# Attention, gated network and relu6 network in one kernel: attention steps placed later and closer in the first block, and x's loads and result copies reordered in the second network

## The chip, the cores and the metric

The kernel runs on one core of one Trainium2 chip. The metric is device microseconds (us) of that core; the kernel before has a median of 1795.02 us over three runs (1794.77 to 1796.37).

A core has five engines that each run their own list of instructions in order and wait for each other through semaphores: TensorE (PE: matmuls, and PEld, its weight loads), VectorE (DVE), ScalarE (ACT), GpSimd (POOL) and SyncE (SP, which here only issues transfers). The profile gives TensorE's granted clock as a share of full speed.

## The reference

Three stages follow each other on 4608 tokens of 512 features:

```
attention: 8 batches, 8 heads, 576 tokens, 64 features a head, in chunks of 64 tokens
  s = q_c @ k_c.T / 8 ;  p = exp(s - max(s)) ;  p = p / (sum(p) + 1e-9) ;  x = p @ v_c
first network (d_ff 1536):
  xn = x / sqrt(mean(x*x) + 1e-6) * rms_g
  y  = (silu(xn @ w_gate) * (xn @ w_val)) @ w_out
second network (d_ff 2048):
  h = y @ w_in ;  out = (h * clip(h + 3, 0, 6) / 6) @ w_out
```

All inputs are float32. Each product is made of three matmuls on split operands (high part times high part, low times high, high times low), so that the result keeps nearly the accuracy of float32.

## The kernel before

The tokens are cut into nine blocks of 512. **The first network** runs over the blocks b = 0 to 8, and in each over twelve steps f of 128 hidden features. A step has three parts: the gate product (`mm_up` into PSUM bank 2, 12 matmuls, then silu on ScalarE into the one buffer `sg`), the value product (`mm_up` into bank 3, then VectorE multiplies it into `sg`, L890, and `split_act` makes the high part `ah` on ScalarE, L746, and the low part `al` on GpSimd, L747), and the down product of the step before (`mm_down_a`, 12 matmuls into banks 4 to 7, of which the last four, L720, read `al`). After each part a counter `hk` (0 to 35) goes up, and two hooks are called with it: `att_hook` and `prep_hook`.

`att_hook` places the attention of the next block, two halves of 256 tokens (class `Pair`), one after the other: `turn` (two transposes of q and k on VectorE), `scores` (TensorE), `top` and `less` (VectorE), `expo` (ScalarE), `total` (VectorE), `share` (GpSimd), `trans_p` (TensorE), `out_p` (ScalarE), `values` (TensorE), `out_x` and `square` (ScalarE) and `squares` (VectorE). When both halves are done, `rms` norms the block, and at the block's end `x_split` writes the high and low parts XH and XL for the next block. In later blocks a half takes five steps f. In block 0 the same distances are kept, one step later: the first half stands at hk 4 to 16 (steps 2 to 6, counted from 1), the second at hk 19 to 31, and `rms` at hk 34.

`prep_hook` prepares in block 0 the 36 weight pieces of the first network. Every second hk issues one stage for two pieces at a time (`Prep.step`): on VectorE the last operation of one group (`lo`, L171) and eight operations of the next (`bits`, L147, L149, L151, L155, two each), on ScalarE a cast and an absolute value (`hi`, L162, `mag`, L140). A stage stands on VectorE directly behind what the hook before it issued. In later blocks the weights of the second network are prepared instead, at a slower pace (`Stash.step`).

**The second network** takes block 0 alone and then pairs of blocks (1 and 2, 3 and 4, 5 and 6, 7 and 8). A pair needs seven sums and differences of its x, each as high and low part (the `xo` tiles, made from `x4` by `x_fill`: four subtractions `xt` on VectorE, then for each operand a cast on ScalarE, L932, and a subtraction on VectorE, L935). `x_fill` is a generator with two rounds c = 0 and 1, which use one buffer `x4` in turn; `go(fill, n)` runs it up to its n-th `yield`. The products of a pair come in eight iterations i (42 matmuls each, L704). While one block's down products of these iterations are collected in one half of PSUM, the gated values of the other block are kept; when the eight are done, two last down products for the first block follow, its results are scaled and copied out (`o_store`, one half by ScalarE, one by VectorE, L761), and sixteen down products for the second block (`mm_down_b`, 12 matmuls each, whose operands `split_act` makes one or two products ahead) run while `x_fill` prepares the next pair. All transfers of x and of the results, and the stream of stored weights (`stream.ahead`), are issued in order by SyncE.

Of the kernel before, what the change touches and what calls it, by code (L numbers as in the profile page):

```python
# [17 lines left out]
def _f32_of(word):  # L18
# [18 lines left out]
    square3 mean2 spread1 norm1 spread0 root2 squares3 mean3 wl2 inv2 root3 wh3 hi1 spread2 norm0 inv3 wm5  # L37
    norm2 hi2 lo1 spread3 hi0 lo2 norm3 hi3 lo3 wh4 wm6 lo0 wl3 wb5 wb6 wh5 wl4
""".split()
STEPS_A = range(0, 36, 2)  # L40


@with_exitstack
def fused_kernel(
# [13 lines left out]
    nc = tc.nc  # L58
# [6 lines left out]
    N = 512  # L65
    NB = NT // N
# [4 lines left out]
    NQ = FB // 2  # L71
# [431 lines left out]
    TP = 256  # L503
# [250 lines left out]
            nc.vector.tensor_copy(t[:, 1, :], PS[:, YB + m + 1, :])  # L754
            nc.sync.dma_start(out=yd[b][:, m:m + 2, :], in_=t)

    def o_store(b, base=YB):
        for m in range(0, NTL, 2):
            t = st_p.tile([128, 2, DM], F32, tag="st", name="ost")
            for z, e in ((0, nc.scalar.mul), (1, nc.vector.tensor_scalar_mul)):  # L760
                e(t[:, z, :], PS[:, base + m + z, :], 1.0 / 6.0)  # L761
                r = b * N + (m + z) * 128
                if b == NB - 1:
                    nc.sync.dma_start(out=out[r:r + 128, :], in_=t[:, z, :])
            r = b * N + m * 128
            if b < NB - 1:
                nc.sync.dma_start(out=out[r:r + 256, :].rearrange("(m p) d -> p m d", p=128), in_=t)
# [11 lines left out]
    with tc.manual_schedule():  # L779
# [38 lines left out]
        def att_hook(b, hk):  # L818

            if b + 1 >= NB:  # L820
                return
            f, o = divmod(hk, 3)
            a = state["att"]
            if b == 0:
                if hk == 0:
                    a.load_v()
                f -= 1
            t, g = divmod(f, 5)
            if t < 0:
                return  # L830
            if t == N // TP:
                if o == 1 and g == 0:
                    rms(b + 1)
                return
            if (g, o) == (0, 1):
                a.run("turn")
                if a.i + 1 < NPR:
                    state["nxt"] = Pair(a.i + 1)
                    if b == 0:
                        state["parts"] = state["nxt"].parts_qk()  # L840
                    else:
                        state["nxt"].load_qk()
            elif (g, o) == (1, 0):
                a.run("scores")
            elif (g, o) == (1, 1):
                a.run("top", "less", "expo")
            elif (g, o) == (2, 1):
                a.run("total", "share")
            elif (g, o) == (3, 1):
                a.run("trans_p", "out_p")  # L850
            elif (g, o) == (4, 1):
                a.run("values", "out_x", "square", "squares")
                if "nxt" in state:
                    state["att"] = state.pop("nxt")
                    state["att"].load_v()

# [56 lines left out]
        def x_fill(b):  # L913

            for j in range(7):
                if j not in X:
                    X[j] = [wp.tile([128, 2, N], F32R, tag="w", name="xo") for _ in range(2)]
            for c in range(2):
                x4 = xf_p.tile([128, KD, N], F32, tag="xf", name="x4")
                nc.sync.dma_start(out=x4[:, 0:2, :], in_=yd[b][:, c:c + 3:2, :])  # L920
                nc.sync.dma_start(out=x4[:, 2:4, :], in_=yd[b + 1][:, c:c + 3:2, :])
                yield
                x11, x21, x12, x22 = (x4[:, z, :] for z in range(4))
                src = {B11: x11, B21: x21, B22: x22}
                for j, p, m in ((T1, x12, x11), (T2, x22, T1), (T3, x22, x12), (T4, x21, T2)):
                    src[j] = tmp_p.tile([128, N], F32, tag="tmp", name="xt")
                    nc.vector.tensor_tensor(src[j], p, src[m] if m in (T1, T2) else m, op=ALU.subtract)  # L927
                    if j == T2 or j == T4:
                        yield
                for j in range(8):  # L930
                    if j < 7:
                        nc.scalar.copy(X[j][0][:, c, :], src[j])  # L932
                    if j > 0:
                        hi, lo = X[j - 1]
                        nc.vector.tensor_tensor(  # L935
                            lo[:, c, :], src[j - 1], hi[:, c, :].bitcast(F32), op=ALU.subtract
                        )
                    yield
# [19 lines left out]
        def relu(r, h):  # L958
            nc.scalar.activation(r, h, AF.Relu, bias=three)
# [29 lines left out]
        for b in range(1, NB, 2):  # L989
# [3 lines left out]
            for i in range(NQ):  # L993
                f0, f1 = 2 * i, 2 * i + 1
                t = [stream.t[i, k_] for k_ in range(4)]
                p0, p1, p2, p3 = (PS[:, base + z, :] for z in range(4))
                add = nc.vector.tensor_tensor
                product(base, t[0][:, 0], X[B11])
                u1 = temp("u1")
                nc.scalar.copy(u1, p0)  # L1000
                product(base + 1, t[0][:, 1], X[T2])
                u2 = temp("u2")
                add(u2, u1, p1, op=ALU.add)  # L1003
                product(base + 2, t[1][:, 1], X[T3])
                u3 = temp("u3")
                add(u3, u2, p2, op=ALU.add)
                product(base + 3, t[1][:, 0], X[T1])
                c22 = temp("c22")
                add(c22, u3, p3, op=ALU.add)
                r22 = g_tile(f1)  # L1010
                relu(r22, c22)
                add(u2, u2, p3, op=ALU.add)
                product(base, t[2][:, 0], X[B21])
                add(u1, u1, p0, op=ALU.add)
                r11 = sg_p.tile([128, N], F32, tag="sg", name="sg")
                relu(r11, u1)
                product(base + 1, t[3][:, 1], X[T4])
                gate(r22, c22)
                add(u3, u3, p1, op=ALU.add)
                r21 = at_p.tile([128, N], F32, tag="sqs", name="r21")  # L1020
                relu(r21, u3)
                product(base + 2, t[2][:, 1], X[B22])
                stream.ahead(4)
                gate(r11, u1)
                add(u2, u2, p2, op=ALU.add)
                r12 = g_tile(f0)
                relu(r12, u2)
                if prev is not None:
                    for z in range(2):
                        mm_down_b(W["out2", f0 - 2 + z], prev[z], i == 1 and z == 0, False, base=yb)  # L1030
                gate(r21, u3)
                gate(r12, u2)
                prev = [split_act(r11), split_act(r21)]
            fill = x_fill(b + 2) if b + 2 < NB else iter(())
            nx = []
            for z in range(2):
                mm_down_b(W["out2", FB - 2 + z], prev[z], False, z == 1, base=yb)
                nx.append(split_act(g_tile(z)))
            o_store(b, yb)
            for f in range(FB):  # L1040
                if 0 < f < FB - 1:
                    nx.append(split_act(g_tile(f + 1)))
# [35 lines left out]
```

## Time and profile before

| | |
|---|---|
| profiled execution | 1796.53 us, its span 1794.7 us |
| runs | 1795.02 us median of 3 |
| granted TensorE clock, mean | 0.984 |
| TensorE matmuls busy | 1729.3 us, 96% of the span |
| VectorE busy | 881.4 us, 49% |
| ScalarE busy | 643.5 us, 36% |
| GpSimd busy | 495.1 us, 28% |
| transfers, share of 16 engines | 31.7% and 7.1% on the two large queues |

The span cut into 40 equal slices (45 us each), as the page prints them: TensorE is at nine tenths or more from the fifth slice on, and below it only in the first four, in which VectorE stands at seven and eight tenths, and the granted clock at seven tenths in the first two.

```
PE   5698999999999999999999999999999999999999
DVE  7886554445455444644542243544554454454440
PEclk7799999999999999999999999999999999999999
```

A row of a timeline gives the start, the length, the engine, the line of the kernel, the operation, what it writes and reads, how many instructions were merged, and in brackets how long the engine stood idle before it and what ended that idle time. Matmuls overlap: one takes 0.39 us as recorded, and the next starts 0.23 us after it.

### The profile page before, as it was taken

What the parts mean: (1) busy time and instruction counts of PE and PEld (TensorE: products, weight loads), DVE (VectorE), ACT (ScalarE), POOL (GpSimd) and SP (SyncE); (2) the same over time, 40 slices, a digit from 0 to 9 for tenths busy, and PEclk for the clock granted to TensorE, in tenths of its full rate; (3) what the DMA queues carried; (4) which work ended last, traced back from release to release, by engine and by line L of the source; (5) the groups of instructions that cost most, each with busy time, mean ns of one, the idle gap of its engine ahead of it and who ended that gap; (6) DMA issues with size and microseconds to landing.
All of it is one profiled execution on the core that took longest, in us unless ns stands there. A gap on an engine that the chain in (4) does not pass through costs nothing.

```text
span 1794.7 us, 24671 instructions
## 1 busy us (share of the span) xinstructions
PE 1729.3 (96%) x9664; PEld 1417.1 (79%) x9664; DVE 881.4 (49%) x1186; ACT 643.5 (36%) x971; POOL 495.1 (28%) x359
## 2 busy tenths in 40 slices
PE   5698999999999999999999999999999999999999
PEld 4577788888888888888888888887788778878887
DVE  7886554445455444644542243544554454454440
ACT  5453333343333333334332133333333333333332
POOL 2321232323323232332333232112421321142123
PEclk7799999999999999999999999999999999999999
DMA  9831342423424133342317354444244334424410
GB/s 268 227 68 29 84 110 69 117 55 97 106 71 125 51 95 95 85 113 77 92 42 262 142 205 147 164 141 141 70 164 141 114 103 141 142 88 141 141 63 32
DMA packets 273589, 207.17 MB, mean 115 GB/s; under 512 B 196289, under 2 KB 233153, under 8 KB 273345
## 3 DMA queue, kind: packets, MB, share of 16 engines
q1 hardware_dynamic: 240704, 163.65, 31.7%
q10 hardware_dynamic: 32768, 41.95, 7.1%
q8 instruction: 76, 1.25, 0.3%
q14 instruction: 41, 0.33, 0.1%
HBM read 161.48 MB, written 44.04 MB: 115 GB/s over the span
## 4 chain that ended last, share of the span: by engine, by line
PE 86%; DVE 6%; DMA 4%; issue 1%; SPq 1%; ACT 1%; POOL 0%; DVEq 0%; POOLq 0%
PE PS L693 32%; PE PS L704 17%; PE PS L725 6%; PE PS L726 6%; PE PS L729 6%; PE PS L717 5%; PE PS L718 5%; PE PS L720 5%; DMA x<-yd 2%; DVE xo L935 1%; PE PS L569 1%; PE PS L629 1%; DVE xt L927 1%; DMA wraw<-in_moe_w_val_dram 1%; PE PS L611 1%
## 5 line engine op out<-in xcount | busy, mean ns | idle before, releaser
L747 POOL TENSOR_TENSOR al<-sg,ah 128x512 fp32r<-128x512 f32 x156 | 213.7, 1370 | 1023.0 <-ACT ah L746 716.1
L693 PE MATMUL PS<-XH,w 128*128 128x512 f32 x1728 | 439.1, 397 | 9.3 <-DVE sg L890 3.2
L693 PEld LDWEIGHTS PS<-XH,w 128*128 128x128 f32 x1728 | 328.1, 191 | 81.9 <-DVE sg L890 3.9
L704 PE MATMUL PS<-xo,wq 128*128 128x512 f32 x1344 | 309.2, 389 | 0.0
L704 PEld LDWEIGHTS PS<-xo,wq 128*128 128x128 f32 x1344 | 252.3, 188 | 52.4
L890 DVE TENSOR_TENSOR sg<-sg,PS 128x512 f32<-128x512 f32 x108 | 74.1, 686 | 336.2 <-PE PS L693 332.2
L725 PE MATMUL PS<-w,ah 128*128 128x512 f32 x576 | 225.2, 391 | 10.7 <-ACT ah L746 10.7
L693 PE MATMUL PS<-XL,w 128*128 128x512 f32 x864 | 233.6, 392 | 0.0
L726 PE MATMUL PS<-w,ah 128*128 128x512 f32 x576 | 224.2, 389 | 0.0
L746 ACT CAST ah<-sg 128x512 fp32r<-128x512 f32 x156 | 96.8, 621 | 293.1 <-DVE sg L890 249.4
L693 PEld LDWEIGHTS PS<-XL,w 128*128 128x128 f32 x864 | 164.2, 190 | 35.3 <-POOL XL L495 0.6
L717 PE MATMUL PS<-ah,w 128*128 128x512 f32 x432 | 174.8, 405 | 0.0
L718 PE MATMUL PS<-ah,w 128*128 128x512 f32 x432 | 168.3, 390 | 0.0
L729 PE MATMUL PS<-w,al 128*128 128x512 f32 x576 | 154.5, 389 | 0.0
L885 ACT ACTIVATE sg<-PS 128x512 f32<-128x512 f32 x108 | 64.5, 597 | 229.3 <-PE PS L693 176.6
L725 PEld LDWEIGHTS PS<-w,ah 128*128 128x128 f32 x576 | 108.1, 188 | 36.8 <-ACT ah L746 14.5
L729 PEld LDWEIGHTS PS<-w,al 128*128 128x128 f32 x576 | 107.8, 188 | 23.0 <-POOL al L747 0.6
L726 PEld LDWEIGHTS PS<-w,ah 128*128 128x128 f32 x576 | 108.1, 188 | 22.3
L720 PE MATMUL PS<-al,w 128*128 128x512 f32 x432 | 115.6, 389 | 1.3 <-POOL al L747 1.3
L1003 DVE TENSOR_TENSOR u<-u,PS 128x512 f32<-128x512 f32 x32 | 22.0, 688 | 156.7 <-PE PS L704 147.6
L717 PEld LDWEIGHTS PS<-ah,w 128*128 128x128 f32 x432 | 81.1, 188 | 18.8 <-issue 1.9
L720 PEld LDWEIGHTS PS<-al,w 128*128 128x128 f32 x432 | 81.0, 188 | 18.5 <-POOL al L747 1.7
(135 smaller groups left out, 1937.3 us busy)
## 6 DMA issues: line engine op xcount, KB each, us to landing
wq<-stash_in SPq DMA_DIRECT2D x152, 512.0 KB, 3.7
yd<-yst SPq DMA_DIRECT2D x18, 512.0 KB, 3.0
sraw<-in_moe_w_in_dram ACTq DMA_DIRECT2D x16, 512.0 KB, 4.7
stash_in<-slo ACTq DMA_DIRECT2D x32, 256.0 KB, 2.9
sraw<-in_moe_w_out_dram ACTq DMA_DIRECT2D x16, 512.0 KB, 5.8
w<-stash_out SPq DMA_DIRECT2D x16, 512.0 KB, 4.1
x<-yd SPq DMA_DIRECT2D x16, 512.0 KB, 5.6
out_dram<-ost SPq DMA_DIRECT2D x16, 512.0 KB, 3.2
```

Of the source, the lines that this page charges most:

```text
L693: nc.tensor.matmul(ps, w(wi, c), xs[c][xi], start=(i == 0), stop=(i == n - 1))
L704: nc.tensor.matmul(PS[:, bank, :], op[:, wi, c * 128:(c + 1) * 128], x[xi][:, c, :], start=(i == 0), stop=(i == 5),)
L717: nc.tensor.matmul(ps, wm[0], a[0], start=first, stop=False)
L718: nc.tensor.matmul(ps, wm[1], a[0], start=False, stop=False)
L720: nc.tensor.matmul(PS[:, YB + m, :], w[:, 0, m * 128:(m + 1) * 128], a[1], start=False, stop=last)
L725: nc.tensor.matmul(PS[:, base + m, :], am, w[:, 0, :], start=first, stop=False)
L726: nc.tensor.matmul(PS[:, base + m, :], am, w[:, 1, :], start=False, stop=False)
L729: nc.tensor.matmul(PS[:, base + m, :], a[1][:, m * 128:(m + 1) * 128], w[:, 0, :], start=False, stop=last)
L746: nc.scalar.copy(hi, t)
L747: nc.gpsimd.tensor_tensor(lo, t, hi.bitcast(F32), op=ALU.subtract)
L885: nc.scalar.activation(s, PS[:, GB, :], AF.Silu)
L890: nc.vector.tensor_tensor(s, s, PS[:, VB, :], op=ALU.mult)
```

## The change

In block 0 a table by hk takes the place of the shifted distances: the first half of the attention stands at hk 13 to 20 and the second at hk 22 to 29, each step as far from the next as the table says, and `rms` at hk 31, where later blocks have it. The later blocks keep their places (`LATER` is the old chain of conditions as a table). The loads of the following half's q and k, which the hook starts at `turn`, and of v, at `squares`, move with them.

In the second network the generator for the next pair is made before the last down products of iteration i = 7, and run once, so that SyncE issues the loads of round 0 there, behind the stream's loads and ahead of the results' transfers. Round 1 rests five more yields between its load and its first subtraction. `o_store` of the first block of a pair makes all four copies on VectorE.

```
+FIRST = {
+    13 + 9 * t + d: steps
+    for t in range(2)
+    for d, steps in (
+        (0, ("turn",)),
...
+        (7, ("values", "out_x", "square", "squares")),
+    )
+}
+FIRST[31] = ("rms",)
...
-    def o_store(b, base=YB):
+    def o_store(b, base=YB, engines=(nc.scalar, nc.vector)):
         for m in range(0, NTL, 2):
             t = st_p.tile([128, 2, DM], F32, tag="st", name="ost")
-            for z, e in ((0, nc.scalar.mul), (1, nc.vector.tensor_scalar_mul)):
-                e(t[:, z, :], PS[:, base + m + z, :], 1.0 / 6.0)
+            for z, e in enumerate(engines):
+                mul = e.mul if e is nc.scalar else e.tensor_scalar_mul
+                mul(t[:, z, :], PS[:, base + m + z, :], 1.0 / 6.0)
...
             if b == 0:
                 if hk == 0:
                     a.load_v()
-                f -= 1
-            t, g = divmod(f, 5)
...
+                due = FIRST.get(hk, ())
+            else:
+                f, o = divmod(hk, 3)
+                t, g = divmod(f, 5)
+                due = LATER.get((g, o), ()) if t < N // TP else ("rms",) if (g, o) == (0, 1) else ()
+            for step in due:
+                if step == "rms":
                     rms(b + 1)
+                    continue
+                a.run(step)
+                if step == "turn" and a.i + 1 < NPR:
                     state["nxt"] = Pair(a.i + 1)
...
                 nc.sync.dma_start(out=x4[:, 2:4, :], in_=yd[b + 1][:, c:c + 3:2, :])
-                yield
+                for _ in range(1 + 5 * c):
+                    yield
...
                 r12 = g_tile(f0)
                 relu(r12, u2)
+                if i == NQ - 1:
+                    fill = x_fill(b + 2) if b + 2 < NB else iter(())
+                    go(fill, 1)
                 if prev is not None:
...
-            fill = x_fill(b + 2) if b + 2 < NB else iter(())
             nx = []
             for z in range(2):
                 mm_down_b(W["out2", FB - 2 + z], prev[z], False, z == 1, base=yb)
                 nx.append(split_act(g_tile(z)))
-            o_store(b, yb)
+            o_store(b, yb, (nc.vector, nc.vector))
```

What stands on VectorE in block 0 from the multiply of step 2 on, before (L890 is the multiply, L556 and L557 the transposes of `turn`, L171 to L155 one preparation stage of two pieces):

```order
L890 TENSOR_TENSOR sg<-sg,PS 128x512
L556 STREAM_TRANSPOSE qT<-q 128x1024
L557 STREAM_TRANSPOSE kT<-k 128x1024
L171 TENSOR_TENSOR w<-wraw,w 128x512 x2
L147 TENSOR_SCALAR wtmp<-wtmp 128x512 x2
L149 TENSOR_SCALAR wtmp<-wtmp 128x512 x2
L151 SCALAR_TENSOR_TENSOR wtmp<-wraw,wtmp 128x512 x2
L155 SCALAR_TENSOR_TENSOR wraw<-wraw,wtmp 128x512 x2
```

The same place in the changed kernel, where the multiply is L902 and the stage L193 to L177, up to the multiply of step 3:

```order
L902 TENSOR_TENSOR sg<-sg,PS 128x512
L193 TENSOR_TENSOR w<-wraw,w 128x512 x2
L169 TENSOR_SCALAR wtmp<-wtmp 128x512 x2
L171 TENSOR_SCALAR wtmp<-wtmp 128x512 x2
L173 SCALAR_TENSOR_TENSOR wtmp<-wraw,wtmp 128x512 x2
L177 SCALAR_TENSOR_TENSOR wraw<-wraw,wtmp 128x512 x2
L193 TENSOR_TENSOR w<-wraw,w 128x512 x2
L169 TENSOR_SCALAR wtmp<-wtmp 128x512 x2
L171 TENSOR_SCALAR wtmp<-wtmp 128x512 x2
L173 SCALAR_TENSOR_TENSOR wtmp<-wraw,wtmp 128x512 x2
L177 SCALAR_TENSOR_TENSOR wraw<-wraw,wtmp 128x512 x2
L902 TENSOR_TENSOR sg<-sg,PS 128x512
```

The transposes are gone from here: two stages stand directly behind the multiply of step 2. The same holds at step 4, where `total` stood between the multiply and two stages, and at step 3, where `top` and `less` stood before one stage.

On VectorE around `total` of the first half, before (L597 to L600 are `total`, then two stages, of which the second is cut here, up to the multiply of step 5):

```order
L597 TENSOR_REDUCE sm<-p 128x16
L598 TENSOR_SCALAR sm<-sm 128x16
L600 RECIPROCAL rs<-sm 128x16
L171 TENSOR_TENSOR w<-wraw,w 128x512 x2
L147 TENSOR_SCALAR wtmp<-wtmp 128x512 x2
L149 TENSOR_SCALAR wtmp<-wtmp 128x512 x2
L151 SCALAR_TENSOR_TENSOR wtmp<-wraw,wtmp 128x512 x2
L155 SCALAR_TENSOR_TENSOR wraw<-wraw,wtmp 128x512 x2
```

Now (L619 to L622 are `total`, L674 is `squares` of the same half):

```order
L619 TENSOR_REDUCE sm<-p 128x16
L620 TENSOR_SCALAR sm<-sm 128x16
L622 RECIPROCAL rs<-sm 128x16
L193 TENSOR_TENSOR w<-wraw,w 128x512 x2
L169 TENSOR_SCALAR wtmp<-wtmp 128x512 x2
L171 TENSOR_SCALAR wtmp<-wtmp 128x512 x2
L173 SCALAR_TENSOR_TENSOR wtmp<-wraw,wtmp 128x512 x2
L177 SCALAR_TENSOR_TENSOR wraw<-wraw,wtmp 128x512 x2
L902 TENSOR_TENSOR sg<-sg,PS 128x512
L674 TENSOR_REDUCE sqs<-kT 128x256
```

Between `total` and `squares` stood three stages and two multiplies; now one stage and one multiply stand there, and `share`, `trans_p`, `out_p`, `values`, `out_x` and `square` on the other engines have that much time.

On SyncE at the end of a pair's iterations (here blocks 3 and 4), before (L324 is the stream of stored weights, L767 the results, L920 and L921 the loads of x):

```order
L324 DMA wq<-stash_in_108 128x1024 x4
L324 DMA wq<-stash_in_111 128x1024 x2
L767 DMA out_dram<-ost 128x2x512 x2
L920 DMA x_11324<-yd_104 128x2x512
L921 DMA x_11324<-yd_105 128x2x512
L920 DMA x_11429<-yd_104 128x2x512
```

Now (L346 the stream, L932 and L933 the loads of x, L790 the results):

```order
L346 DMA wq<-stash_in_108 128x1024 x4
L346 DMA wq<-stash_in_111 128x1024 x2
L932 DMA x_11250<-yd_104 128x2x512
L933 DMA x_11250<-yd_105 128x2x512
L790 DMA out_dram<-ost 128x2x512 x2
L932 DMA x_11429<-yd_104 128x2x512
```

The two loads of round 0 have moved in front of the results' transfers, and follow the stream's loads at once.

## Rows read from the trace of the kernel before

**Rows 1.** TensorE by stretch: length, busy and matmuls, granted clock, transfers' share, GB/s
```profile
55.60:190.10 134.50, 117.55 (x706) 0.92 0.38 94
1123.53:1142.57 19.04, 19.04 (x86) 1.00 0.64 221
1243.21:1291.24 48.03, 44.55 (x193) 1.00 0.21 66
1410.93:1459.43 48.50, 44.56 (x194) 1.00 0.21 66
1579.11:1626.91 47.80, 44.53 (x194) 1.00 0.21 66
```

**Rows 2.** TensorE's waits: line, releaser, us in total, times, longest
```profile
PE PS L725 <- ACT ah L746: 10.7, 9, 1.5
```

**Rows 3.** Timeline of TensorE in block 0 and at the start of block 1
```profile
81.77 1.98 PE L569 MATMUL PS<-kT,qT 64*64 64x64 f32 x64 [3.21 <-DVE kT L557]
...
115.19 3.61 PE L693 MATMUL PS<-XH,w 128*128 128x512 f32 x8 [3.15 <-DVE sg L890]
...
139.99 1.99 PE L569 MATMUL PS<-kT,qT 64*64 64x64 f32 x64 [5.27 <-DVE kT L557]
...
190.10 0.50 PE L693 MATMUL PS<-XH,w 128*128 128x512 f32 x1 [2.02 <-ACT XH L682]
...
199.46 1.98 PE L693 MATMUL PS<-XH,w 128*128 128x512 f32 x8
```

**Rows 4.** Timeline of VectorE in block 0
```profile
68.42 1.28 DVE L171 TENSOR_TENSOR w<-wraw,w 128x512 fp32r<-128x512 f32 x2
...
72.17 1.29 DVE L155 SCALAR_TENSOR_TENSOR wraw<-wraw,wtmp 128x512 uint32<-128x512 uint32 x2
75.25 0.69 DVE L890 TENSOR_TENSOR sg<-sg,PS 128x512 f32<-128x512 f32 x1 [1.78 <-ACT sg L885]
75.85 1.24 DVE L556 STREAM_TRANSPOSE qT<-q 128x1024 f32<-128x1024 f32 x1
...
92.10 1.22 DVE L579 TENSOR_REDUCE mx<-PS 128x16 f32<-128x1024 f32 x1
93.36 1.29 DVE L589 TENSOR_TENSOR p<-PS,mx 128x512 f32<-128x512 f32 x2
...
100.56 1.21 DVE L597 TENSOR_REDUCE sm<-p 128x16 f32<-128x1024 f32 x1
...
102.90 2.93 DVE L171 TENSOR_TENSOR w<-wraw,w 128x512 fp32r<-128x512 f32 x2
...
114.46 0.68 DVE L890 TENSOR_TENSOR sg<-sg,PS 128x512 f32<-128x512 f32 x1
...
125.11 2.06 DVE L652 TENSOR_REDUCE sqs<-kT 128x256 f32<-128x1024 f32 x1 [2.52 <-ACT kT L649]
```

**Rows 5.** Timeline of GpSimd in block 0
```profile
69.24 5.35 POOL L747 TENSOR_TENSOR al<-sg,ah 128x512 fp32r<-128x512 f32 x1 [9.99 <-ACT ah L746]
76.67 1.30 POOL L747 TENSOR_TENSOR al<-sg,ah 128x512 fp32r<-128x512 f32 x1 [2.09 <-ACT ah L746]
...
103.06 2.22 POOL L605 TENSOR_TENSOR p<-p,rs 128x1024 f32<-128x1024 f32 x1 [0.40 <-DVE rs L600]
```

**Rows 6.** Timeline of ScalarE in block 0, and in the second network at blocks 1 and 2
```profile
77.60 1.21 ACT L140 ACTIVATE wtmp<-wraw 128x512 f32<-128x512 f32 x2
...
1251.20 0.62 ACT L932 CAST xo<-x 128x512 fp32r<-128x512 f32 x1 [5.30 <-DMA x<-yd]
```

**Rows 7.** Timeline of SyncE's issues in block 0, and in the second network
```profile
138.84 16.25 SPq L537 DMA_DIRECT2D q<-in_q_dram  x32
...
1210.76 22.55 SPq L324 DMA_DIRECT2D wq<-stash_in  x8
...
1244.76 0.79 SPq L920 DMA_DIRECT2D x<-yd  x1
```

**Rows 8.** Timeline of VectorE in the second network, at the first subtraction of x
```profile
1252.58 1.67 DVE L927 TENSOR_TENSOR xt<-x 128x512 f32<-128x512 f32 x1 [8.33 <-DMA x<-yd]
```

More of the change, by code (lines that the diff above doesn't have):

```diff
@@ L39 @@
 """.split()
+FIRST = {
[3 more added lines that the diff above has]
+        (0, ("turn",)),
+        (2, ("scores",)),
+        (3, ("top", "less", "expo")),
+        (4, ("total", "share")),
+        (6, ("trans_p", "out_p")),
+        (7, ("values", "out_x", "square", "squares")),
+    )
+}
+FIRST[31] = ("rms",)
+LATER = {
+    (0, 1): ("turn",),
+    (1, 0): ("scores",),
+    (1, 1): ("top", "less", "expo"),
+    (2, 1): ("total", "share"),
+    (3, 1): ("trans_p", "out_p"),
+    (4, 1): ("values", "out_x", "square", "squares"),
+}
 STEPS_A = range(0, 36, 2)
@@ L821, in att_hook @@
                 return
-            f, o = divmod(hk, 3)
             a = state["att"]
@@ L826, in att_hook @@
                     a.load_v()
-                f -= 1
-            t, g = divmod(f, 5)
[L829 to L832, printed above, removed]
+                due = FIRST.get(hk, ())
[5 more added lines that the diff above has]
+                if step == "rms":
                     rms(b + 1)
[L834 to L837, printed above, removed]
+                    continue
+                a.run(step)
+                if step == "turn" and a.i + 1 < NPR:
                     state["nxt"] = Pair(a.i + 1)
@@ L842, in att_hook @@
                         state["nxt"].load_qk()
[L843 to L853, printed above, removed]
+                elif step == "squares" and "nxt" in state:
                     state["att"] = state.pop("nxt")
```

## The prediction, made blind

> **What bounds the kernel now.** I read the stretches of TensorE first, then its waits, then the timelines of the engines that it waits for. TensorE is busy nearly all the time, so a gain is there only where it stands or runs slowly. In undisturbed work 84 matmuls take 19.04 us, 0.2267 us each (the second stretch of [rows 1], which counts two overlapping neighbours with them). Two places fall short of that.
>
> The first is block 0. Its 36 products of 12 matmuls are 432 x 0.2267 = 97.9 us, and the stretch takes 134.5 at a mean granted clock of 0.92 [rows 1]. TensorE stands 3.21 and 5.27 us for the transposed k, 3.15 us for a multiply and 2.02 us for XH at the start of block 1 [rows 3]. After each of the four the clock is at its lower level for a while: eight matmuls at 115.19 are recorded with 3.61 us, against 1.98 for the same eight at 199.46 [rows 3]. At the start of block 1, 24 matmuls from 190.10 end at 199.46, 9.36 us instead of 5.44, so this spell cost 3.9.
>
> What stands behind these waits is VectorE. One preparation stage goes from 68.42 to 73.46, 5.0 us (its first and last instruction stand in [rows 4]); three stages fall on two steps of TensorE. With the multiply of 0.6 that is 8.1 us a step against 36 x 0.2267 = 8.16 of TensorE. Any attention put in between makes VectorE the bound as long as the stages last.
>
> There is a second hold. After the multiply of step 1, the low part on GpSimd took 5.35 us, from 69.24 to 74.59, and that of step 2 only 1.30 [rows 5]. The first began while a stage ran on VectorE and ended 1.13 after it; the second ran while VectorE transposed [rows 4]. The same 5.4 us stands at 115.87, one multiply of step 5 (114.46) and one stage later; these two of twelve are the only long ones. A low part that comes behind the stage's first instruction thus waits for the whole stage. `sg` has one buffer, so silu of the next step waits for that low part, and the next multiply for silu: VectorE stood 1.78 us until 75.25 [rows 4].
>
> The second place is the start of the sixteen down products of a pair of blocks. Three stretches of 192 matmuls take 48.03, 48.50 and 47.80 us [rows 1], 144.3 against 3 x 43.5 = 130.6: 13.7 us. In each TensorE waits three times for the high part from ScalarE, 10.7 us in all [rows 2]; the rest is refilling behind the waits. ScalarE itself stands in a cast of x that waits 5.30 us for a transfer, with the casts for TensorE behind it [rows 6]; VectorE waits 8.33 for the same loads [rows 8]. They are issued only at 1244.76, though the stream ahead of them was done at 1210.76 + 22.55 = 1233.3 [rows 7].
>
> **The second network, priced.** The two loads of round 0 move to 1233.3, 11.4 us earlier, and the subtraction could begin at 1252.58 - 11.4 = 1241.2, before the down products that end about 1243.2. The casts and subtractions then find x there. Two of three waits go. For the third: round 0's last operands now stand beside the fifth product, so the buffer is free and round 1's loads go out about 1243.2 + 4.7 x 2.72 = 1256; a pair of loads took 1252.58 - 1244.76 = 7.8 us [rows 7, 8], so x is there about 1264; with the extra yields the first subtraction stands at the ninth product, 1243.2 + 8 x 2.72 = 1265. I take this wait as hidden too, by a small margin. The generator now needs 26 turns after the first, 13 of 16 products at two a product, so it still ends in time; in block 0's single pass it needs 27 of 30. Those later copies cost nothing there, as long as ScalarE keeps up with TensorE.
>
> The two copies that move to VectorE cost 0.6 us each there (a multiply from PSUM is 0.69 recorded [rows 4]), 1.2 a pass in front of the first subtraction, and free ScalarE by as much. No one waits for them: 1241.2 plus the four copies from 1243 is about 1245.5, where the first cast of x stood in the order anyway. Bounds for what remains: 0 (all waits go) to 1.5 us a pass, if GpSimd's low part is held by four subtractions and three operand copies of 0.6 in a row (4.2 us, against a slack of one product, 2.72). I take 0.25 a pass: **-13.0 us**, bounds -13.7 and -9.2.
>
> **Block 0, priced.** Nothing is removed; the same instructions stand elsewhere. I follow the multiplies, since the value product of the next step needs each. From one multiply to the next it is 0.6 + 5.0 a stage + 1.8 (low part, silu) when the stages stand directly behind it.
> - Step 2: 75.25 as before. Now two stages follow without the transposes, and the low part is held through both: step 3 at 75.25 + 0.6 + 9.9 + 1.8 = 87.6. TensorE has finished its high matmuls about 82.9 and waits for the low part till 87, 4 us, and then runs slowly.
> - Step 4: one stage, 7.4, and 1.1 more for the slow clock and for ScalarE, whose casts and absolute values (1.21 a couple [rows 6]) now come behind the late silu: 96.1. Step 5: two stages, 12.4: 108.5, against 114.46 before [rows 4]. TensorE waits 2 us more for the low part of step 4.
> - Step 6: the two transposes (1.2 each) give GpSimd its window; 0.6 + 2.4 + 1.1 + 5.0: 117.6.
> - Step 7: `top` and `less` 2.5, a stage, `total` 2.35 (100.56 to 102.90), a stage that loses 1.65 to `share` (2.93 instead of 1.28) [rows 4], 0.6: 134.7. TensorE's value product is over by 123.5 to 125; `total` ends at 128.0, `share` takes 2.22 more [rows 5], and the transposes of p stand ahead of the down product in TensorE's order: a new wait of 5.5 to 7 us. From `top` to `trans_p` three products lie in that order now, where six lay.
> - Step 8: cast, copy, `values`, two readings by ScalarE, `squares` (2.06 with a wait of 2.52 ahead of it before [rows 4]) and a stage, 12.8: 147.5. Step 9: transposes, one and a quarter stages, 9.2: 156.7.
> - The second `trans_p`: 0.6 + 2.5 + 2.0 (the exponential, an estimate: two 512 columns on ScalarE are 1.21 [rows 6], and two hand-overs) + 2.35 + 2.4 for `share` behind that: 166.5, a wait of some 3.5.
> - Then ten products of 2.72, the small matmuls 2.5, and 2.8 for the slow clock behind that wait (between the 1.6 at 115.19 and the 3.9 at 190.10): 199.0. `rms` is three hooks earlier and has three products more of cover, so neither the 2.02 us at XH nor the 3.9 behind it comes back.
>
> Before, the same matmul stood at 199.46 [rows 3]. That is -0.5 us: the waits for k and for XH go, and waits for the low part and for `share` come. I take **-0.5**, with bounds from -8 (no low part held, the waits for p half as long) to +4 (every spell of slow clock as long as the longest seen).
>
> The moved loads: 64 small ones of the next half are issued behind the second `turn`, 16.25 us for 32 [rows 7], so from 150 to 183; `turn` of block 1 comes near 199. The sixteen loads of v and then the stores of y queue behind them till about 191; the buffers of these stores are wanted by ScalarE's loads in step 2 of block 1. I price this at nothing; if the cover failed, ScalarE would be held by the 2 to 3 us by which they overlap.
>
> **A rule against the trace.** By the rows GpSimd is shut out for a whole stage once the stage has passed its first instruction [rows 4, 5]. The Trainium skill (SBUF — State Buffer, "Who interferes with whom") has the port that VectorE and GpSimd share as a lock that is held for one instruction, by whoever issues first. By it a low part would come in after one instruction of 0.6 us. At 103.06 `share` did, behind the stage's first instruction [rows 4, 5]; at 69.24 it did not. The result by that rule is the first rival.
>
> **The rivals.**
> 1. GpSimd gets in at the next boundary of two instructions. The low parts then cost VectorE 1.3 instead of 1.8 of idling, silu is early, the 4 us at step 3 and its slow clock go, and the multiplies stand 4 to 5 us earlier from step 5 on; the waits for p stay. Block 0 gains 5.5: 1795.0 - 13.0 - 5.5 = 1776.5. The row of `share` speaks for it, the two long low parts, which began at the same distance from their multiply as now, against.
> 2. Slower: TensorE's clock doesn't come back between the new waits. With waits of 4, 2, 5.5 and 3.5 us from 83 to 166, some six steps of 49 us would run at half speed and take 98; the waits (15) and the spells (9) already counted lie in that. That is 49 - 24 = +25 in block 0, and 1795.0 - 13.0 - 0.5 + 25 = 1806.5. It decides once the clock is still low when the next wait comes. Against: the longest spell of before cost 3.9 us, and by 199.46, 9.4 us behind its wait, the matmuls were fast again [rows 3].
> 3. The early loads change little, because GpSimd, held by the run of subtractions, makes the low parts late instead, or because the round 1 wait stays: half of 13.7 is kept, 1788. Against: in the rows the wait is ScalarE's and VectorE's for a transfer, and GpSimd has a product of slack.
>
> **How the numbers follow.** The sum is made against the profiled execution, 1796.5 us with 1.8 outside its span; the median of the runs is 1.5 lower, 1795.0, and I take the difference from that: 1795.0 - 13.0 - 0.5 = **1781.5**. Chances: forecast 0.53 (own range 1777.5 to 1787), rival 1 0.30, rival 3 0.10, rival 2 0.03, and 0.04 for more than these. Range 1772 to 1788. A change within 0.2% (3.6 us) can't be told from none. Rivals 1 and 3 and the forecast are all faster; with a slip in block 0 of ten microseconds on top of rival 3 it would be the same: faster 0.93, same 0.03, slower 0.04.
>
> **What would show it.** Right: the three stretches of 192 matmuls near 43.7 us, the loads of x issued some 10 us before the results' transfers, no wait of TensorE for the high part there; low parts of steps 2 and 4 on GpSimd of 9 us or more; the multiply of step 3 near 87.6 and that of step 5 near 108.5; a wait of about 5 us for `share` ahead of the transposes of p; block 1 starting without a wait for XH. Wrong: low parts of 1.3 us all through block 0 (rival 1), a granted clock near one half from 83 to 166 (rival 2), or casts of x that still wait for a transfer (rival 3).

## The result, and the profile after

| | before | after |
|---|---|---|
| median of the runs compared | 1795.46 us (1794.77 to 1796.37, 4 runs) | 1777.67 us (1774.17 to 1778.53, 4 runs) |
| ratio | | 0.9893, 95% interval 0.9876 to 0.9910 |
| profiled execution, its span | 1796.53, 1794.7 | 1774.17, 1772.3 |
| TensorE matmuls busy | 1729.3 us | 1720.1 us |
| granted TensorE clock, mean | 0.984 | 0.987 |

The change saves 17.8 us by the medians. 13.5 were forecast. The time, 1777.7, lies in the stated range (1772 to 1788), at the fast end of the forecast's own range (1777.5 to 1787). The profiled execution of after is its fastest run, 3.5 us below the median, and that of before lies 1.1 above its own, so the two traces differ by 22.4.

Where they differ, by stretches of TensorE in after: block 0 from its first matmul to the third product of block 1, and the three stretches of sixteen down products in the second network (length, busy time and matmuls, granted clock, transfers' share, GB/s):

```profile
55.49:190.97 135.48, 120.51 (x731) 0.94 0.40 100
1234.71:1278.39 43.68, 43.68 (x194) 1.00 0.14 49
1397.90:1441.60 43.70, 43.70 (x194) 1.00 0.14 49
1561.10:1604.79 43.69, 43.69 (x194) 1.00 0.14 48
```

Block 0 of before, between the same two matmuls:

```profile
55.62:199.46 143.84, 126.75 (x731) 0.90 0.38 96
```

The three stretches took 48.03, 48.50 and 47.80 us [rows 1] and are now filled to the last matmul: 13.3 us. Block 0 gives 8.4. Together that is 21.7 of the 22.4.

In the second network the timelines of SyncE, ScalarE and VectorE in after (start, length, engine, line, operation; in brackets the idle time ahead and what ended it) answer to [rows 6 to 8]:

```profile
1224.87 0.53 SPq L932 DMA_DIRECT2D x<-yd  x1
1225.44 0.61 SPq L933 DMA_DIRECT2D x<-yd  x1
...
1235.55 1.58 SPq L790 DMA_DIRECT2D out_dram<-ost  x2
...
1237.59 0.62 ACT L945 CAST xo<-x 128x512 fp32r<-128x512 f32 x1
...
1246.17 0.53 SPq L932 DMA_DIRECT2D x<-yd  x1
...
1252.44 0.74 DVE L940 TENSOR_TENSOR xt<-x 128x512 f32<-128x512 f32 x1 [4.59 <-DMA x<-yd]
```

The loads of round 0 go out 10.7 us ahead of the results, and the first cast of x (L945) no longer stands for a transfer. For round 1 VectorE still stands 4.59 us, but TensorE does not wait for it there: TensorE's wait for `ah`, 10.7 us in all before [rows 2], is gone from its list.

In block 0, TensorE's timeline in after:

```profile
74.50 1.21 PE L742 MATMUL PS<-al,w 128*128 128x512 f32 x4 [1.23 <-POOL al L769]
...
93.54 1.19 PE L742 MATMUL PS<-al,w 128*128 128x512 f32 x4 [1.25 <-POOL al L769]
...
108.79 1.99 PE L591 MATMUL PS<-kT,qT 64*64 64x64 f32 x64 [3.17 <-DVE kT L579]
110.71 2.77 PE L715 MATMUL PS<-XH,w 128*128 128x512 f32 x8
...
126.59 1.97 PE L633 MATMUL PS<-ident,p 128*128 128x128 f32 x8 [4.03 <-POOL p L627]
...
160.60 1.09 PE L633 MATMUL PS<-ident,p 128*128 128x128 f32 x8 [2.06 <-POOL p L627]
...
185.53 1.98 PE L715 MATMUL PS<-XH,w 128*128 128x512 f32 x8
...
190.97 1.98 PE L715 MATMUL PS<-XH,w 128*128 128x512 f32 x8
```

The waits for k of 3.21 and 5.27 us, for the multiply (3.15) and for XH [rows 3] have become one of 3.17 for k and two for `share`, 4.03 and 2.06, with some short ones. Block 1 (185.53) starts without a wait and at the full clock. GpSimd's timeline in after shows what the forecast had otherwise, the low parts of steps 1 to 4 (L769):

```profile
69.10 5.34 POOL L769 TENSOR_TENSOR al<-sg,ah 128x512 fp32r<-128x512 f32 x1 [9.99 <-ACT ah L768]
76.53 1.63 POOL L769 TENSOR_TENSOR al<-sg,ah 128x512 fp32r<-128x512 f32 x1 [2.08 <-ACT ah L768]
88.14 5.35 POOL L769 TENSOR_TENSOR al<-sg,ah 128x512 fp32r<-128x512 f32 x1 [9.98 <-ACT ah L768]
95.57 1.63 POOL L769 TENSOR_TENSOR al<-sg,ah 128x512 fp32r<-128x512 f32 x1 [2.09 <-ACT ah L768]
```

And VectorE's multiplies (L902) of steps 2 to 5, 7 and 9:

```profile
75.11 0.69 DVE L902 TENSOR_TENSOR sg<-sg,PS 128x512 f32<-128x512 f32 x1 [1.78 <-ACT sg L897]
76.92 1.86 DVE L169 TENSOR_SCALAR wtmp<-wtmp 128x512 f32<-128x512 f32 x2
...
86.73 0.68 DVE L902 TENSOR_TENSOR sg<-sg,PS 128x512 f32<-128x512 f32 x1
94.15 0.69 DVE L902 TENSOR_TENSOR sg<-sg,PS 128x512 f32<-128x512 f32 x1 [1.78 <-ACT sg L897]
105.78 0.68 DVE L902 TENSOR_TENSOR sg<-sg,PS 128x512 f32<-128x512 f32 x1
...
130.76 0.68 DVE L902 TENSOR_TENSOR sg<-sg,PS 128x512 f32<-128x512 f32 x1
...
152.27 0.68 DVE L902 TENSOR_TENSOR sg<-sg,PS 128x512 f32<-128x512 f32 x1
```

At steps 1 and 3 the low part was held for a whole stage, as in [rows 5]. At steps 2 and 4 it came in after 1.63 us; the 1.86 us of L169 at 76.92 (0.76 at 69.49) is VectorE standing aside for it. The forecast had 9 us or more there.

### The profile page after: what moved, and what is told of

Same layout as the page of the kernel before. It is cut to its first block, busy times and chain, and to the rows that moved or that the text cites. A ratio compares the mean times of both kernels' runs of the same rounds, so it can differ in the third digit from the quotient of the medians.

```text
span 1772.3 us, 24676 instructions
## 1 busy us (share of the span) xinstructions
PE 1720.1 (97%) x9664; PEld 1414.5 (80%) x9664; DVE 885.8 (50%) x1194; ACT 640.9 (36%) x963; POOL 490.1 (28%) x359
## 3 DMA queue, kind: packets, MB, share of 16 engines
q8 instruction: 76, 1.25, 0.3%
## 4 chain that ended last, share of the span: by engine, by line
PE 90%; DVE 5%; issue 1%; POOL 1%; DMA 1%; SPq 1%; ACT 0%; DVEq 0%; POOLq 0%
PE PS L715 32%; PE PS L726 17%; PE PS L748 7%; PE PS L751 7%; PE PS L747 7%; PE PS L739 5%; PE PS L740 5%; PE PS L742 5%; PE PS L591 1%; PE PS L651 1%; PE PS L633 1%; DVE w L193 1%; DVE wtmp L173 1%; DVE wtmp L169 1%; DVE wraw L177 1%
## 5 line engine op out<-in xcount | busy, mean ns | idle before, releaser
L769 POOL TENSOR_TENSOR al<-sg,ah 128x512 fp32r<-128x512 f32 x156 | 214.6, 1376 | 1011.1 <-ACT ah L768 707.3
L715 PE MATMUL PS<-XH,w 128*128 128x512 f32 x1728 | 432.2, 392 | 4.3 <-ACT XH L514 1.9
L715 PEld LDWEIGHTS PS<-XH,w 128*128 128x128 f32 x1728 | 324.3, 189 | 74.0 <-ACT XH L514 2.2
L902 DVE TENSOR_TENSOR sg<-sg,PS 128x512 f32<-128x512 f32 x108 | 74.0, 685 | 320.1 <-PE PS L715 309.2
L751 PEld LDWEIGHTS PS<-w,al 128*128 128x128 f32 x576 | 108.1, 188 | 22.4
L748 PEld LDWEIGHTS PS<-w,ah 128*128 128x128 f32 x576 | 108.1, 188 | 22.4
L747 PEld LDWEIGHTS PS<-w,ah 128*128 128x128 f32 x576 | 108.1, 188 | 22.4
L739 PEld LDWEIGHTS PS<-ah,w 128*128 128x128 f32 x432 | 81.7, 189 | 18.9 <-issue 1.9
```

What stands on the lines that cost most here:

```text
L715: nc.tensor.matmul(ps, w(wi, c), xs[c][xi], start=(i == 0), stop=(i == n - 1))
L739: nc.tensor.matmul(ps, wm[0], a[0], start=first, stop=False)
L747: nc.tensor.matmul(PS[:, base + m, :], am, w[:, 0, :], start=first, stop=False)
L748: nc.tensor.matmul(PS[:, base + m, :], am, w[:, 1, :], start=False, stop=False)
L751: nc.tensor.matmul(PS[:, base + m, :], a[1][:, m * 128:(m + 1) * 128], w[:, 0, :], start=False, stop=last)
L769: nc.gpsimd.tensor_tensor(lo, t, hi.bitcast(F32), op=ALU.subtract)
```

## The experiments

The theory after the result had three parts. The early loads, and not the other two edits, give the second network's gain. Block 0 gains some 7 us where 0.5 were forecast, because the low parts of steps 2 and 4 come in and the spells at the lower clock are shorter. What is left there are waits that VectorE's order sets. Times are medians, ratios are to the kernel before on the same chip.

**Each half alone.** Block 0 alone puts the three edits of the second network back as they were; the second network alone gives the table the old distances:

```
e2_second_only:
-    13 + 9 * t + d: steps
+    4 + 15 * t + d: steps
...
-        (4, ("total", "share")),
-        (6, ("trans_p", "out_p")),
-        (7, ("values", "out_x", "square", "squares")),
+        (6, ("total", "share")),
+        (9, ("trans_p", "out_p")),
+        (12, ("values", "out_x", "square", "squares")),
...
-FIRST[31] = ("rms",)
+FIRST[34] = ("rms",)
```

> Only the part in block 0 (the table and rms at hk 31), with the second network as before. My theory from the two traces: the second product of block 1 ended 8.4 us earlier after the change, in a run that was some 3.5 us faster than the others, so block 0 alone gives 4 to 8.5 us: 1787 to 1791.5. The forecast on record gave this part -0.5: 1795. Rival: the gain of block 0 is worth its 8.4 us only together with the second network: no rival mechanism for that is known, it would show as less than 3 us here.

> Only the part in the second network, with block 0's attention at its old places. Theory: the nine waits for the high part go, 13.7 us: 1781.7, and block 0's waits stay as before (3.2, 3.2, 5.3 and 2.0 us). Rival: part of the gain of the whole change comes from the shift in time between the two networks, then this falls short of 13 us.

Block 0 alone: 1787.37, ratio 0.9958 (0.9944 to 0.9972), 7.8 us faster. Its TensorE still waits for the high part in the second network (line, releaser, us in total, times, longest):

```profile
PE PS L747 <- ACT ah L768: 9.2, 10, 1.4
```

The second network alone: 1783.47, ratio 0.9935 (0.9922 to 0.9947), 11.7 us faster. Its TensorE keeps the two waits for k, and its down products are filled:

```profile
PE PS L591 <- DVE kT L579: 14.0, 9, 6.6
```

```profile
1243.70:1287.40 43.70, 43.70 (x195) 36.19 (x194) 25.81 (x27) 16.91 (x30) 20.78 (x15) 1.00 0.14 49
```

Its block 0, in the old order:

```profile
56.06:199.15 143.09, 121.75 (x730) 0.93 0.38 97
```

That is nearly as long as in the kernel before (143.84), though the same matmuls were busy 5.0 us less (121.75 against 126.75) at a higher mean clock (0.93 against 0.90): TensorE stood 4.3 us longer instead. So shorter spells at the lower clock are not by themselves a gain, and that block 0 gained by them is not shown.

The halves add up within the noise: 7.8 and 11.7 are 19.5, against 16.9 to 18.9 for the kernels with both (next run, and the three below with the second network's other edits undone). So block 0 was worth about 7, not 0.5.

**The changed kernel once more**, beside these.

> The changed kernel again, to see what its run-to-run difference of 4 us is. Theory: the low parts on GpSimd come in or not, or TensorE's clock stays low longer behind one of the waits in block 0; the span differs in block 0 alone, and the second product of block 1 ends between 191 and 195 us. Rival: the difference is in the start (loads) before 55.5 us.

1778.22, ratio 0.9904 (0.9891 to 0.9918). Its profile shows where profiles of one order differ by some microseconds. First TensorE behind the wait for k, then its row of block 0 as a whole:

```profile
110.37 1.99 PE L591 MATMUL PS<-kT,qT 64*64 64x64 f32 x64 [3.17 <-DVE kT L579]
112.29 3.78 PE L715 MATMUL PS<-XH,w 128*128 128x512 f32 x8
```

```profile
57.08:195.25 138.17, 121.92 (x731) 0.93 0.40 100
```

Here the eight matmuls behind the wait take 3.78 us, the lower level (1.2 GHz) throughout (granted clock 0.50 from 112.29 to 116.00); in the first profile of after (110.71) they took 2.77, part at the lower and part at the higher level (2.4 GHz; granted clock 0.73 from 110.71 to 113.40). Of the 5.3 us between the two spans, 2.7 lie in block 0. 1.6 lie ahead of it (its first matmul starts at 57.08 here and at 55.49 there), as the expectation's rival had it. Over the seven profiles with block 0 as changed and nothing else edited in it, block 0 takes 134.4 to 138.3 us, 136.7 in the mean, against 143.8 and 143.1 in the two with the old order. That is a gain of 7 with a spread of 4 from run to run. Over the seven, the same matmuls are busy between 119.2 and 122.8 us, so most of the spread goes with the clock.

**Spare silu buffers in block 0**: silu and the multiply of the first six steps use the four quarters of the idle x buffer in turn, in place of the one buffer `sg` (`KD` is 4).

```
+            if b == 0:
+                spare = xf_p.tile([128, KD, N], F32, tag="xf", name="sgx")
...
-                s = sg_p.tile([128, N], F32, tag="sg", name="sg")
+                if b == 0 and f < 6:
+                    s = spare[:, f % KD, :]
+                else:
+                    s = sg_p.tile([128, N], F32, tag="sg", name="sg")
```

> The changed kernel, but silu of steps 1 to 6 of block 0 writes into quarters of the idle x buffer, so that it doesn't wait for the low part of the step before. Theory H (GpSimd gets the port between two instructions of a stage only where VectorE has just waited): the multiply of step 2 no longer waits, so the low part of step 2 is held through two stages, 8 us or more, and TensorE waits about 4 us for it; total within 3 us of the changed kernel. Theory G (GpSimd gets in where it has worked shortly before): the low part of step 2 follows that of step 1 at once and takes under 2 us, the 1.78 us that VectorE stood at steps 2 and 4 go, and the total is 2 to 4 us lower, about 1774.

1773.50, ratio 0.9876 (0.9863 to 0.9890): 4.7 us under the changed kernel run beside it. VectorE's multiplies and GpSimd's low parts of steps 1 and 2:

```profile
68.80 0.67 DVE L907 TENSOR_TENSOR sgx<-sgx,PS 128x512 f32<-128x512 f32 x1
...
70.20 5.39 POOL L769 TENSOR_TENSOR al<-sgx,ah 128x512 fp32r<-128x512 f32 x1 [9.98 <-ACT ah L768]
...
74.35 0.68 DVE L907 TENSOR_TENSOR sgx<-sgx,PS 128x512 f32<-128x512 f32 x1
...
75.76 1.55 POOL L769 TENSOR_TENSOR al<-sgx,ah 128x512 fp32r<-128x512 f32 x1 [0.16 <-ACT ah L768]
```

The hold at step 1 stays, but silu no longer waits for it, so VectorE goes from stage to multiply without the 1.78 us. It also settles one theory: VectorE did not stand at all before step 2, and the low part still came in. So a pause of VectorE is not what lets GpSimd in.

**The three edits of the second network, one by one.**

```
e5_late_loads:
-                if i == NQ - 1:
-                    fill = x_fill(b + 2) if b + 2 < NB else iter(())
-                    go(fill, 1)
...
+            fill = x_fill(b + 2) if b + 2 < NB else iter(())
e6_no_rests (also in e9):
-                for _ in range(1 + 5 * c):
-                    yield
+                yield
e10_copies_as_before (also in e9):
-            o_store(b, yb, (nc.vector, nc.vector))
+            o_store(b, yb)
```

> The changed kernel with one of its three edits in the second network undone: the loads of round 0 are issued behind the results' transfers again (the five extra rests of round 1 and the copies on VectorE stay). If the early loads carry the gain, the first two of the three waits of each pass come back, two thirds of 13.7 us: 1778 + 9 = 1787, PE waiting for ah about nine times two thirds, 6 times, some 7 us. If the copies on VectorE carry it, by freeing ScalarE, the time stays within 2 us of 1778.

> The changed kernel without the five extra rests of round 1 (early loads and copies on VectorE stay). In the changed kernel round 1's loads go out at 1246.17, because the buffer is free only then, and VectorE still stands 4.59 us for them at 1252.44. If the rests are needed, ScalarE meets the first cast of round 1 two and a half products (6.8 us) earlier and stands for the transfer with casts for TensorE behind it: one wait a pass, three in all, 1778 + 4.6 = 1782.6. If the casts made one product ahead cover it, nothing changes: within 1.5 us of 1778.

> The changed kernel with two of the three edits of the second network undone: no extra rests of round 1, and the first block's copies on ScalarE and VectorE by turns again. Only the early loads of round 0 stay (and block 0 as changed). If the early loads alone carry the gain, the time is that of the changed kernel, 1778 within 2 us, and TensorE has no wait for ah. If they need the copies on VectorE too, ScalarE's copies (0.6 us each, two a pass) stand ahead of the casts for TensorE and one wait a pass comes back: 1778 + 4.6 = 1782.6.

> The changed kernel with the first block's copies on ScalarE and VectorE by turns again (early loads and extra rests stay). If the copies on VectorE are worth nothing, 1778 within 2 us; if they save ScalarE two copies of 0.6 us a pass on TensorE's path, 1778 + 4 = 1782. Where the early loads alone come out slow, this run tells whether the copies or the rests are missed.

| | median, us | ratio and interval | TensorE's wait for `ah` |
|---|---|---|---|
| late loads | 1787.75 | 0.9954 (0.9941 to 0.9966) | 7.2 us, 5 times |
| no rests | 1777.12 | 0.9899 (0.9884 to 0.9914) | none |
| early loads alone | 1776.74 | 0.9894 (0.9880 to 0.9909) | 0.6 us, once |
| copies as before | 1776.57 | 0.9896 (0.9879 to 0.9912) | none |

With late loads, SyncE and ScalarE show the old chain again:

```profile
1239.76 1.58 SPq L790 DMA_DIRECT2D out_dram<-ost  x2
1241.38 0.53 SPq L932 DMA_DIRECT2D x<-yd  x1
...
1248.06 0.62 ACT L945 CAST xo<-x 128x512 fp32r<-128x512 f32 x1 [6.17 <-DMA x<-yd]
```

Ten microseconds come back, as the early loads' theory had it (1787). It is then no faster than block 0 alone (1787.37). The other two edits are worth nothing that can be measured, singly or together. Without the rests, ScalarE and VectorE at round 1 show why:

```profile
1253.22 0.62 ACT L944 CAST xo<-x 128x512 fp32r<-128x512 f32 x1
...
1254.52 0.98 DVE L939 TENSOR_TENSOR xt<-x 128x512 f32<-128x512 f32 x1 [4.35 <-DMA x<-yd]
...
1256.26 1.14 ACT L944 CAST xo<-xt 128x512 fp32r<-128x512 f32 x2 [0.22 <-DVE xt L939]
```

ScalarE's first cast of round 1 comes behind casts for TensorE and does not stand for the transfer. VectorE waits 4.35 us, but ScalarE stands only 0.22 us for its subtraction, and no cast for TensorE comes late by it. The third wait of a pass, which the extra rests were to hide, thus went with the early loads: without the rests round 1's loads go out at 1248.49, in the kernel before at 1263.12, behind the late round 0.

**The transposes of p one hook later**, and with them `values` and `rms`:

```
-        (6, ("trans_p", "out_p")),
-        (7, ("values", "out_x", "square", "squares")),
+        (7, ("trans_p", "out_p")),
+        (8, ("values", "out_x", "square", "squares")),
...
-FIRST[31] = ("rms",)
+FIRST[32] = ("rms",)
```

> The changed kernel with transposes of p, values and rms one hook later in block 0. If the waits for share (4.03 and 2.06 us) are TensorE's own, they go with the slow clock behind them (some 2 us): 1778 - 6 = 1772 or a little above. If VectorE's list is the bound there, the time returns at once as longer waits for multiplies and transposed k, and the kernel stays within 1.5 us of 1778.

1773.63, ratio 0.9875 (0.9861 to 0.9888), some 4 us under the changed kernel. TensorE's waits of 4.03 and 2.06 become 1.26 and none, and one new wait follows the first:

```profile
129.07 1.09 PE L633 MATMUL PS<-ident,p 128*128 128x128 f32 x8 [1.26 <-POOL p L627]
...
135.54 1.16 PE L651 MATMUL PS<-qT,v 64*64 64x64 f32 x64 [2.61 <-ACT qT L639]
```

ScalarE at the same place:

```profile
133.95 0.62 ACT L768 CAST ah<-sg 128x512 fp32r<-128x512 f32 x1 [2.50 <-DVE sg L902]
134.48 1.01 ACT L639 COPY qT<-PS 128x1024 f32<-128x1024 f32 x1
```

So a part of these waits was TensorE's own: of 6.09 us, 1.26 stay, and 2.61 come back ahead of `values`: the copy of the transposed p stands on ScalarE behind the cast of `ah`, and that stood for VectorE's multiply. The 6 us of the expectation were a little too many, and its rival (VectorE's list gives all of it back) falls. The low part of step 7, 1.28 us in after, now meets a stage and is held:

```profile
134.65 5.37 POOL L769 TENSOR_TENSOR al<-sg,ah 128x512 fp32r<-128x512 f32 x1 [5.63 <-ACT ah L768]
```

**A version that beats both**: this, the first `turn` one hook earlier, and the spare buffers.

```
+FIRST[12] = FIRST.pop(13)
```

> Block 0 with three edits on top of the changed kernel: the transposes of p, values and rms one hook later, the first turn one hook earlier (which gives the transposed k three more microseconds against a wait of 3.17), and six silu buffers in place of one (experiment with six buffers: 4.7 us). If each wait costs what TensorE shows, 1778 - 4.7 - 4 - 3 = 1766, at the best. If VectorE's and GpSimd's work in block 0 bounds it, no more than the six buffers give: 1773.

1768.23, ratio 0.9849 (0.9836 to 0.9862): 27.2 us under the kernel before. The two expectations were 1766 and 1773; it is nearer the first. Block 0 and what is left of the wait for k in it:

```profile
55.41:183.98 128.57, 117.52 (x730) 0.97 0.41 100
```

```profile
PE PS L592 <- DVE kT L580: 4.0, 8, 1.1
```

The changed kernel's block 0 takes 136.7 in the mean; of the difference of 8.1, 4.7 were the spare buffers' and some 4 the later steps', each taken alone. That leaves nothing for the earlier `turn`, for which 3 us were expected; no run has it alone.

**Which low parts are held.** The low part of step 2 goes to VectorE, and GpSimd has nothing to do between steps 1 and 3:

```
-    def split_act(t):
+    def split_act(t, low=nc.gpsimd):
...
-        nc.gpsimd.tensor_tensor(lo, t, hi.bitcast(F32), op=ALU.subtract)
+        low.tensor_tensor(lo, t, hi.bitcast(F32), op=ALU.subtract)
...
-                a = split_act(s)
+                a = split_act(s, nc.vector if b == 0 and f == 1 else nc.gpsimd)
```

> The changed kernel with the low part of step 2 of block 0 made on VectorE instead of GpSimd; all other low parts as in the changed kernel. GpSimd then stands idle from the end of step 1's low part (held) to step 3's, some 13 us. Three theories of which low parts are held through a stage. By idleness (held after several idle microseconds, not shortly after another operation), step 3's is held again, 5.3 us, and step 4's comes in, 1.6. By turns (an operation whose forerunner was held comes in), step 3's comes in, 1.6 us, and step 4's is held. By the prediction's theory (every one that meets the stage behind its first instruction) both are held. Time: VectorE works 0.6 us more and waits 0.7 for the high part behind the multiply, but step 3's silu waits for VectorE and not for GpSimd: 1778 within 3 us by all three.

1777.70, ratio 0.9898 (0.9883 to 0.9912). The low parts of steps 1 to 4:

```profile
70.21 5.35 POOL L769 TENSOR_TENSOR al<-sg,ah 128x512 fp32r<-128x512 f32 x1 [9.98 <-ACT ah L768]
...
77.59 0.69 DVE L769 TENSOR_TENSOR al<-sg,ah 128x512 fp32r<-128x512 f32 x1 [0.69 <-ACT ah L768]
...
89.59 5.28 POOL L769 TENSOR_TENSOR al<-sg,ah 128x512 fp32r<-128x512 f32 x1 [14.04 <-ACT ah L768]
...
96.95 1.63 POOL L769 TENSOR_TENSOR al<-sg,ah 128x512 fp32r<-128x512 f32 x1 [2.09 <-ACT ah L768]
```

Step 3's is held though its forerunner was held too, and step 4's comes in. The theory by turns falls, and the prediction's; of the three, only idleness gave both rows. A fourth was not tested: in every run the held low parts stand behind the multiply of an odd step, where one stage follows, and those let in behind that of an even step, where two follow.

## Why the prediction was right, and where not

**The second network** was right, mechanism and size: -13.0 forecast, 13.3 in the stretches of the traces, 11.7 between medians with that half alone. Two of the steps behind it were needless. The third wait was not hidden by the rests (no rests: the same time), and the copies on VectorE do nothing for ScalarE that shows.

**Block 0** was right in kind (the waits for k and XH go, waits for `share` come, one row of VectorE's work sets the pace) and mis-sized: -0.5 forecast, -8.4 in this trace (just beyond the bound of -8), -7 in the mean of seven. That the time still lies within the range is owed to the range's width. The step that failed is "the low part is held through both" stages at steps 2 and 4: they were let in and took 1.63 us each. Against the multiplies forecast:

| | forecast | measured | earlier by |
|---|---|---|---|
| step 3 | 87.6 | 86.73 | 0.9 |
| step 4 | 96.1 | 94.15 | 2.0 |
| step 5 | 108.5 | 105.78 | 2.7 |
| step 7 | 134.7 | 130.76 | 3.9 |
| step 9 | 156.7 | 152.27 | 4.4 |
| second transposes of p | 166.5 | 160.60 | 5.9 |
| third product of block 1 | 199.0 | 190.97 | 8.0 |

The first 2.7 us lie where the two holds did not come (1.1 of it is the slow clock and ScalarE's casts that were priced behind the first); nor did the 4 and 2 us for which TensorE was to wait for them (its waits of 1.23 and 1.25 are for the low parts of steps 1 and 3). 1.7 more accrue from step 6 to step 9, in small pieces. 1.5 is the second wait for `share`, 2.06 instead of 3.5. The last 2.1 is the spell of slow clock priced at 2.8 behind that wait: the eight matmuls at 165.47 took 2.11 us. So the term was off in several places, and the low parts are a third of it.

The first wait for `share` was sized too long: 4.03 against 5.5 to 7. The moved loads of q, k and v, priced at nothing, cost nothing that shows: outside the two places only 0.7 of the 22.4 us remain.

**Rival 1** (block 0 gains 5.5, 1776.5) came nearer to the time than the forecast, with half its mechanism, so its nearness is in part luck. The Trainium skill (SBUF — State Buffer, "Who interferes with whom") gives the shared ports to whoever issues first "for the whole instruction". The low parts of steps 2 and 4 came in at such a boundary, as that rule has it. Those of steps 1 and 3 were held through eight instructions of VectorE, 5.3 us as recorded against 1.3 at step 5, which the rule does not give.

The forecast told `share`, which came in, from the long low parts by the place where each met the stage. At steps 2 and 4 the low part came at the same place as at steps 1 and 3 (1.4 us behind the multiply) and was let in, so place in the stage does not decide among low parts. GpSimd's idle time before, 0.40 us for `share` and 9.99 for the low part [rows 5], does not explain `share` either. In after, it came in behind 7.17 us of idling, more than the 5.63 ahead of the low part that was held in the run with later transposes of p:

```profile
124.38 2.16 POOL L627 TENSOR_TENSOR p<-p,rs 128x1024 f32<-128x1024 f32 x1 [7.17 <-DVE rs L622]
```

Why some low parts are held and others not stays open.

**Rival 2** (the clock stays low between the waits) did not come: the clock of block 0 rose from 0.90 to 0.94 between the same two matmuls. **Rival 3** (early loads change little) fell with the first trace.

## What to carry to other kernels

A load that an in-order queue issues behind a result's transfer waits for the result's producer; issue it ahead where its buffer is free, and test the edits made beside it one by one, since two of three did nothing here. Where one engine's order bounds a stretch, place the steps that other engines wait for by that engine's list, hook by hook: two moves by one hook and the spare buffers gave another 9 us together. And when a sum rests on a repeated stall, look at every occurrence of it and at every non-occurrence, with all that stands in their rows, before it is multiplied.

## What the runs showed of the hardware

A GpSimd low part (128x512, both operands in SBUF) that starts inside a stage of VectorE, 1.4 to 1.5 us behind the multiply, was either let in (1.55 and 1.63 us) or held to the run's end (5.3 to 5.4 us). Among these low parts GpSimd's idle time before differs: those let in had 0.16, 2.08 and 2.09 us, those held 5.63, 9.98, 9.99 and 14.04. But the step differs too (even and odd, as said above), and `share`, which meets the stage in its first instruction, came in at 7.17 us. So these runs do not tell whether idleness decides; none changed the idle time without moving work.

TensorE's clock behind one and the same wait differs from run to run: behind 3.17 us for k, eight matmuls took 2.77 us in one profile and 3.78 in the next (granted clock 0.73 and 0.50). Such spells go with most of the 4 us by which block 0 differs between profiles of the new order. Between two profiles of the old order, 5.0 us less busy time made block 0 only 0.7 us shorter.
